# Attention and a two-layer product on one core: the first tile's transfers and constants reordered, mask products on their own, seven half-size products from tile 7 on

## The chip, the cores and the metric

The kernel runs on one core of one Trainium2 chip. The metric is the device time of one execution in microseconds, the median of several runs. The engines have short names in the profile: PE is TensorE (matmul), PEld its weight load, DVE is VectorE, ACT is ScalarE, POOL is GpSimd, SP is SyncE, which only issues transfers here.

## The reference

What must be computed is an attention with two kinds of heads, followed by two matrix products with a pointwise function between them:

```python
B, H, S, D = 4, 8, 768, 64          # batch, heads, sequence, head dimension
scores = q @ k.T / sqrt(D)
causal = i >= j
stream = causal & ((j < 4) | (i - j < 64))       # 4 sink positions, a window of 64
mask = causal if is_retrieval[h] else stream     # a flag of each head
a = softmax(where(mask, scores, -1e9))
x = (a @ v)  ->  (B * S, H * D) = (3072, 512)    # all heads of a token side by side
h = x @ w_in                                     # 512 -> 2048
g = h - tanh(h)
out = g @ w_out                                  # 2048 -> 512, float32
```

Inputs and output are float32. The flags are data, so the kernel finds out on the chip which heads are of which kind.

## The kernel before

The 3072 tokens are cut into 12 tiles of 256 tokens (`TT`), three tiles to a batch (`NG`), tile t = 3b + g. All matmuls are in float16. For one tile the steps are:

- **Load q, k, v.** The first tile's q and k come over SP in four transfers (`load_first`, two halves of four heads, q and k each) and are cast by `cast_first`. Tiles 1 and 2 come over GpSimd's queue, cast on the way, packed with two tokens to a row (`load_cast`, tile `t16p`), and `in_order` sorts them into `t16`. From tile 3 on, raw float32 tiles come over SP in two halves (`load_raw`, `rawqk`, `rawv`), and GpSimd casts and sorts the heads by kind (`gather`, lines L654 and L690). Both buffers exist twice.
- **Transpose q and k.** Tiles 0 to 2 on PE (`st_T`, L987) with copies out of PSUM (L968 and L970, tile `QK`); from tile 3 on by a transposing transfer on SP (`turn`, L573).
- **Scores** on PE (`st_S`, L1082), one visit for one to three units of a head pair. In tiles 0 and 1 (`MASKS`) the mask is added in PSUM first, by a matmul of the identity with a mask tile `m4` of the head pair (L1071). In later tiles VectorE multiplies the mask in after the exp.
- **Exp** on ScalarE (L1095, tiles `pt` and `ptn`), then the product with v on PE (`st_A`, L1174), the division by the sums on VectorE (L1194, L1206, L1221), and a transposition of the result into `xT`: on PE for tiles 0 and 1 (`st_X`, L1256), by a transfer for the others (`st_X_tile`, L1238).
- **First product**, `H_unit` (L1298): eight units of a tile, each 8 matmuls of 256 columns; tanh on ScalarE (L1310), g on VectorE (L1317).
- **Second product.** Up to tile `ST - 1` in the plain way (`O_group`, L1356): for each half of the tokens 16 matmuls of 512 columns. From tile `ST` = 8 on (`quick`) with seven half-size products instead of eight, after Strassen and Winograd: the sums of weight parts are made once (`combine`, L1396, results in `t2`, in the place of tile 2's `t16p` and `gu`, and in `wout` itself), the sums of parts of g once per tile (`sums`, L1446), `piece` (L1478) is one product of 8 matmuls of 256 columns, and `take`, `fold` and `add` (L1513, L1532, L1543) put the output together; `send` (L1563) stores it. `step` spreads a tile's pieces over the eight units of the next tile's first product by the table `STEPS`; `finale` does it for the last tile.

Nothing of the order on the engines is written out by hand. Each step is recorded by `op` or `dma` with its engine, a cost in ns, what it reads and what it writes. `Plan.run` then plays the plan through with these costs: each engine takes, of the operations that are ready, the one recorded first; transfers share the rings and land after a `lag`; PSUM banks and buffers come free as their users end. The order that comes out is the order in which the instructions are issued, and each engine works in it. Where PE would have nothing to do in the first 18 us of the plan, products on a tile of ones (L1765) fill the gap. The numbers above `program` say where in the sequence of product slots the loads, gathers, attention steps and weight sums are recorded: `CUT1` for batch 1, `LEAD`, `LD` and `GA` (visit, load, gather) for batches 2 and 3, `TWHEN` and `TQ` for the weight sums (when, and in how many parts each), `CASTS`, `TE`, `XE` (which engine copies what), `ORDER` (GpSimd's early transfers).

Of the kernel before, what the change touches and what calls it, by code (L numbers as in the profile page):

```python
# [11 lines left out]
XS = 4096.0  # L12
# [243 lines left out]
def kernel(  # L256
# [12 lines left out]
    nc = tc.nc  # L269
# [102 lines left out]
    FROM = 3  # L372
# [3 lines left out]
    MSE = 'DVE'  # L376
    FRONT = "A40"
    LATE = [('vf', 0, 3, 0)]
    BEHIND = []
    MASKS = 2  # L380
    AH = 60
    TL = (1100, 1500)
    RL = (700, 1000)
    A2 = (3, 6)
    ORDER = ('t1', 0, 'v1', 1, 2, 4, 3, 5, 't2', 'r3', 6, 7)

    def program(first):
# [56 lines left out]
        def batch(b):  # L444
            if b in QKs:
                return
            QKs[b], v1s[b], vfs[b], kcs[b] = (buf(x)[0] for x in ("QK", "v1", "vf", "kc"))
            op(
                "POOL", 190, lambda: nc.gpsimd.memset(v1s[b]()[:, :, :, D : D + 1], 1.0 / XS),
                w=[("v1", b, blk, x) for blk in range(2 * NG) for x in range(2)],  # L450
            )
# [5 lines left out]
        def load_first():  # L457

            batch(0)
            rq, iq = buf("rawqk")  # L460
            c, ic = buf("t16")
            raws[0], t16s[0] = (rq, iq), (c, ic)
            r4 = lambda: rq()[:].rearrange("p (x h e) -> p x h e", x=2, h=H)
            for half in range(2):
                hs = slice(half * HH, half * HH + HH)
                for x, src in enumerate((q, k)):
                    dma(
                        "SP", 520,
                        lambda x=x, src=src, hs=hs: nc.sync.dma_start(
                            out=r4()[:, x, hs, :],  # L470
                            in_=src[0, hs, 0:TT, :].rearrange("h (p i) d -> p h (i d)", i=2),
                        ),
                        128 * HH, 26.0, w=[("rawqk", iq, x, half)], lag=(700, 1000),
                    )

# [24 lines left out]
        def load_v(t):  # L500

            b, g = divmod(t, NG)
            for i in range(NB):
                blk = g * NB + i
                dma(
                    "POOL", 900,
                    lambda i=i, blk=blk: nc.gpsimd.dma_start(  # L507
                        out=v1s[b]()[:, blk, :, 0:D],
                        in_=v[b, :, blk * 128 : blk * 128 + 128, :].rearrange("h p d -> p h d"),
                    ),  # L510
                    128 * H, 15.5, w=[("v1", b, blk, x) for x in range(2)],
                )

        def load_cast(t):
# [22 lines left out]
            for x, src in enumerate((q, k)):  # L537
                dma(
                    "POOL", 950,
                    lambda x=x, src=src: nc.gpsimd.dma_start(  # L540
                        out=pk()[:].rearrange("p (x h e) -> p x h e", x=2, h=H)[:, x, :, :],
                        in_=src[b, :, g * TT : (g + 1) * TT, :].rearrange(
                            "h (p i) d -> p h (i d)", i=2
                        ),
                    ),
                    128 * H, 22.6, w=[("t16p", ip, x)],
                )
# [5 lines left out]
        def in_order(t):  # L553

            (pk, ip), (c, ic) = packed[t], t16s[t]
            for x in range(2):
                op(
                    "DVE", 500,
                    lambda x=x: nc.vector.tensor_copy(
                        out=c()[:].rearrange("p (x i h d) -> p x i h d", x=2, i=2, h=H)[:, x],  # L560
                        in_=pk()[:].rearrange("p (x h i d) -> p x i h d", x=2, h=H, i=2)[:, x],
                    ),
                    r=[("t16p", ip, x)] + (BEHIND if t == 1 and first else []),
                    w=[("t16", ic, x, half) for half in range(2)], port=True,
                )

# [51 lines left out]
        def load_w_in(j):  # L618
            dma(
                "POOL", 780,  # L620
                lambda: nc.gpsimd.dma_start(  # L621
                    out=w_in_t[j][:],
                    in_=moe_w_in[:, j * 512 : (j + 1) * 512].rearrange("(cb p) f -> p cb f", p=128),
                ),
                512, 78.0, w=[("win", j)],
            )

        def load_w_out(half, part):
# [8 lines left out]
                ),  # L637
                1024, 43.0, w=[("wout", half, part)],
            )
# [111 lines left out]

        def select(m, src, fill, base, step, mult, key, cmp=ALU.is_ge):
            op(
                "POOL", 300,
                lambda: nc.gpsimd.affine_select(
                    out=m, in_=src, compare_op=cmp, fill=fill,
                    base=base, pattern=[[step, 128]], channel_multiplier=mult,
                ),
                r=["ones", key], w=[key],
            )  # L760

        def rank_constants():
            op(
                "POOL", 300,
# [4 lines left out]
                ),  # L769
                r=["ones"], w=["upto"],  # L770
            )

            select(mS[64:128, 3, :], ones[64:128, :], 0.0, window_i - 65, -1, 1, "mS3")
            select(mS[0:64, 3, :], ones[0:64, :], 0.0, n_sink_i - 1, 0, -1, "mS3")


        def constants():
# [248 lines left out]
        def st_S(units):  # L1026

            todo, reads, keys, ns = [], [], [], 160
            for n, gi in units:
# [28 lines left out]
                if gi == 0 and t < MASKS:  # L1058
                    reads.append(("m4", hp))
                    ns += 2 * o * 0.427 + 100  # L1060
                todo.append((n, gi, b, g, hp, near, sc, key, pieces, o))

            def mm():
                for n, gi, b, g, hp, near, sc, key, pieces, wid in todo:
                    QK = QKs[b]()
                    added = gi == 0 and n // HP < MASKS
                    for hh in range(2) if added else ():
                        m = m4[:, 2 * hp + hh, 0:384]
                        if g:
                            m = m4[:, 2 * hp + hh, 256:512].unsqueeze(1).to_broadcast([128, 2, 256])  # L1070
                        nc.tensor.matmul(  # L1071
                            out=sc()[:, hh, 0:wid], lhsT=ident16[:], rhs=m, start=True, stop=False,
                        )
                    for jb, q0, nb, o, comp in pieces:
# [381 lines left out]
        def piece(t, p, beside=None):  # L1456
# [11 lines left out]
                7: (S(3), T(3), summed(2) + both(3)),  # L1468
            }[p]
            po, key = outs[t, p] = outs[t, beside] if beside else bank(  # L1470
                [128, DM], FP32, "one", f"p{t}_{p}"
# [100 lines left out]
        def step(t, i):  # L1572

            for what in STEPS.get(i, ()):
                if what == "a":
# [15 lines left out]
        def finale(t):  # L1591
# [3 lines left out]
            piece(t, 4)  # L1595
            take(t, 4, "F", 0, CM)
            piece(t, 2)
            fold(t, 2, "A", 0, "E", 0, CM)
# [69 lines left out]
        if first:  # L1668
# [128 lines left out]
        if first and fast:  # L1797
            spread_over([by_rank], BR, BR)
            qs = quads()
            spread_over(qs[: 4 * TQ], slot_of[TWHEN[0]], slot_of[TWHEN[1]])  # L1800
            spread_over(qs[4 * TQ :], slot_of[TWHEN[2]], slot_of[TWHEN[2]])
        spread_over(att_pairs(1) + [lambda: scale_v(1, SV)], 0, 0)
# [3 lines left out]
        def point(h):  # L1806
            t, ts = divmod(h, 2)
            return slot_of[t, 4 * ts + 3] if t >= 2 else max(0, 13 + 2 * h)

# [69 lines left out]
        if quick(last):  # L1879
            sums(last)  # L1880
            finale(last)
        else:
# [46 lines left out]
```

## Time and profile before

| what | value |
|---|---|
| three runs | 229.57, 229.90, 230.34 us, median 229.9 us |
| profiled execution | 230.39 us, span from the first to the last instruction 228.7 us |
| granted TensorE clock, mean | 0.995 |
| PE, DVE, ACT, POOL busy | 95%, 72%, 62%, 47% of the span |
| mean rate of the transfers | 154 GB/s |

Times in the profile are microseconds from the span's start, unless marked ns. A row of the timeline gives start, length, engine, line, operation, output<-input and shape; the brackets at its end say how long the engine sat idle before it and what released it. A row of a group gives the count, the busy time, the mean of one in ns, and the idle time before them. A row of the chain of waits gives start, length, engine and line of one piece. Matmuls overlap in the array, so a row of x8 can be longer than the time it takes up in the chain. SPq, POOLq and ACTq rows are transfers being issued, not their data.

### The profile page before, as it was taken

How to read it: one execution, taken by the hardware profiler on the slowest of the kernel's cores; microseconds unless marked ns; L12 is line 12 of the kernel's file. 1: busy time of each engine (PE TensorE's matmuls, PEld its weight loads, DVE VectorE, ACT ScalarE, POOL GpSimd, SP SyncE). 2: the span in 40 equal slices, each digit the busy share in tenths (PEclk: the TensorE clock that was granted, in tenths of full speed). 3: DMA queues.
4: the chain of work that ended last, by engine and by line, in shares of the span. 5: the costliest groups of instructions: out<-in, count | busy, mean ns of one | idle time of the engine just before them, and what ended most of it. 6: DMA issues, size and time to landing. Idle time of an engine off the chain costs nothing.

```text
span 228.7 us, 6301 instructions
## 1 busy us (share of the span) xinstructions
PE 217.4 (95%) x2373; PEld 163.0 (71%) x2373; DVE 165.7 (72%) x401; ACT 140.8 (62%) x219; POOL 108.4 (47%) x241
## 2 busy tenths in 40 slices
PE   6889999999998989999999999999999999999991
PEld 2356787788985666765765767675868889888880
DVE  5777867775674954999986565476789599684891
ACT  3739849977466847746376657655883766732620
POOL 8999343764741908769473919381000021032020
PEclk9999999999999999999999999999999999999997
DMA  5999999999999989999999989947031022022032
GB/s 164 152 190 204 202 193 218 216 176 248 194 180 217 175 171 239 190 249 174 254 184 220 244 201 215 216 107 162 3 92 49 0 49 93 3 47 95 0 108 84
DMA packets 103876, 35.31 MB, mean 154 GB/s; under 512 B 90658, under 2 KB 101922, under 8 KB 103842
## 3 DMA queue, kind: packets, MB, share of 16 engines
q1 hardware_dynamic: 86544, 27.14, 60.5%
q0 software_dynamic: 17152, 7.60, 25.5%
q8 instruction: 19, 0.31, 0.6%
q14 instruction: 15, 0.12, 0.2%
q10 hardware_dynamic: 146, 0.13, 0.2%
HBM read 27.26 MB, written 6.29 MB: 147 GB/s over the span
## 4 chain that ended last, share of the span: by engine, by line
PE 65%; DMA 14%; POOL 8%; ACT 3%; DVE 3%; SPq 3%; issue 2%; POOLq 0%; DVEq 0%
PE banks L1298 26%; PE banks L1356 19%; PE banks L1478 10%; DMA wout<-in_moe_w_out_dram 7%; PE banks L1082 5%; PE banks L1174 5%; DMA rawqk<-in_k_dram 4%; DMA QK<-t 2%; POOL t L654 2%; POOL v L507 2%; ACT pt L1095 2%; SPq L573 1%; POOL win L621 1%; SPq L609 1%; POOL t16p L540 1%
## 5 line engine op out<-in xcount | busy, mean ns | idle before, releaser
L1298 PE MATMUL banks<-xT,win 128*128 128x256 f16 x768 | 94.8, 273 | 0.5 <-DVE gt L1317 0.4
L1298 PEld LDWEIGHTS <-win 128*128 128x128 f16 x768 | 73.0, 98 | 15.9 <-issue 1.6
L1310 ACT ACTIVATE th<-banks 128x512 f32<-128x512 f32 x96 | 57.2, 605 | 38.7 <-PE banks L1298 38.3
L1317 DVE SCALAR_TENSOR_TENSOR gt<-th,banks 128x512 f16<-128x512 f32 x88 | 59.5, 681 | 18.3 <-ACT th L1310 17.3
L1095 ACT ACTIVATE pt<-banks 128x768 f16<-128x768 f32 (+1 forms) x60 | 53.0, 922 | 10.8 <-PE banks L1082 10.5
L1356 PE MATMUL banks<-wout,gt 128*128 128x512 f16 (+1 forms) x288 | 57.0, 332 | 0.2 <-DMA wout<-in_moe_w_out_dram 0.2
L654 POOL CAST t<-rawqk 128x256 f16 x72 | 28.5, 443 | 31.1 <-DMA rawqk<-in_k_dram 24.8
L1356 PEld LDWEIGHTS <-gt 128*128 128x128 f16 x288 | 25.8, 98 | 14.1 <-issue 1.4
L1543 POOL TENSOR_TENSOR ot<-gu,ot 128x256 f32<-128x256 f32 x6 | 4.5, 752 | 56.4 <-ACT gu L1513 41.8
L1206 DVE TENSOR_TENSOR x16t<-banks,rinv 128x128 f32 (+1 forms) x80 | 22.4, 285 | 1.1
L1082 PE MATMUL banks<-QK 64*128 64x128 f16 (+1 forms) x364 | 21.0, 238 | 1.9 <-DMA QK<-t 1.2
L690 POOL CAST v<-rawv 128x128 f16 x72 | 22.3, 356 | 0.0
L1082 PEld LDWEIGHTS <-QK 64*128 64x128 f16 x364 | 12.8, 94 | 10.9 <-issue 8.1
L1095 ACT ACTIVATE ptn<-banks 128x1024 f16<-128x1024 f32 (+1 forms) x18 | 17.2, 953 | 3.6 <-DVE x16t L1206 2.4
L1174 PEld LDWEIGHTS <-pt 128*128 128x128 f16 x420 | 15.9, 97 | 4.4 <-ACT pt L1095 1.1
L1174 PE MATMUL banks<-v,pt 128*128 128x65 f16 x220 | 16.4, 193 | 0.4 <-DVE pt L1145 0.2
L1145 DVE TENSOR_TENSOR pt<-pt,m4r 128x1024 f16<-128x1024 f16 (+1 forms) x18 | 12.5, 694 | 5.8 <-ACT pt L1095 5.8
L1330 ACT ACTIVATE ot<-banks 128x512 f32<-128x512 f32 (+1 forms) x20 | 10.5, 524 | 9.2 <-PE banks L1356 7.9
L1117 DVE TENSOR_TENSOR ptn<-ptn,mS 128x1024 f16<-128x1024 f16 x12 | 9.6, 803 | 7.6 <-ACT ptn L1095 7.4
L1478 PEld LDWEIGHTS <-m 128*128 128x128 f16 x128 | 12.2, 98 | 1.7 <-issue 0.2
L1174 PE MATMUL banks<-vf,pt 128*128 128x65 f16 x200 | 13.1, 193 | 0.3 <-ACT pt L1095 0.3
L1194 DVE RECIPROCAL rinv<-banks 128x4 f32<-128x4 f32 x48 | 8.1, 174 | 5.6 <-PE banks L1174 5.0
(105 smaller groups left out, 234.7 us busy)
## 6 DMA issues: line engine op xcount, KB each, us to landing
rawqk<-in_q_dram SPq DMA_DIRECT2D x18, 256.0 KB, 4.1
rawqk<-in_k_dram SPq DMA_DIRECT2D x18, 256.0 KB, 4.6
out_dram<-ot SPq DMA_DIRECT2D x18, 256.0 KB, 2.6
rawv<-in_v_dram SPq DMA_DIRECT2D x16, 256.0 KB, 4.8
win<-in_moe_w_in_dram POOLq DMA_DIRECT2D x4, 512.0 KB, 10.7
wout<-in_moe_w_out_dram POOLq DMA_DIRECT2D x4, 512.0 KB, 13.0
out_dram<-ot SPq DMA_DIRECT2D x11, 128.0 KB, 4.0
v<-in_v_dram POOLq DMA_DIRECT2D x6, 128.0 KB, 8.1
```

The lines of the kernel that those rows point to most:

```text
L654: nc.gpsimd.tensor_copy(out=c5()[:, :, :, s_ : s_ + 1, :], in_=r5()[:, :, :, at, :])
L690: nc.gpsimd.tensor_copy(out=v1s[b]()[:, g * NB : g * NB + NB, RANK[s_] : RANK[s_] + 1, 0:D], in_=rv()[:, :, at, :],)
L1082: nc.tensor.matmul(out=sc()[:, hh, o : o + nb * 128], lhsT=lhsT, rhs=QK[p_, hp, q_0 : q_0 + nb * 128], start=not added, stop=not added or ...
L1095: lambda pt=pt, sc=sc, gi=gi, wid=wid: nc.scalar.activation(out=pt()[:, :, 512 * gi : 512 * gi + wid], in_=sc()[:, :, 0:wid], func=AF.Exp, ...
L1145: nc.vector.tensor_mul(out=pv, in0=pv, in1=m)
L1174: nc.tensor.matmul(out=av()[:, i, hh, :], lhsT=pt()[:, hh, co : co + 128], rhs=vv, start=(jb == first_jb), stop=(jb == qb),)
L1206: nc.vector.tensor_mul(out=xt()[:, :, at, :], in0=av()[:, :, hh : hh + 1, 0:D], in1=rinv()[:, :, hh : hh + 1].unsqueeze(3).to_broadcast([1 ...
L1298: nc.tensor.matmul(out=ph()[:, j, :], lhsT=w_in_t[fb // 4][:, cb, f0 : f0 + 128], rhs=x, start=(cb == 0), stop=(cb == HP - 1),)
L1310: lambda: nc.scalar.activation(out=th()[:], in_=ph()[:], func=AF.Tanh, scale=1.0 / XS),
L1317: lambda: nc.vector.scalar_tensor_tensor(out=gt()[:, u * FU : (u + 1) * FU, :], in0=th()[:], scalar=-XS, in1=ph()[:], op0=ALU.mult, op1=AL ...
L1356: nc.tensor.matmul(out=po()[:, c0:c1], lhsT=gt()[:, f, ts * 128 : ts * 128 + 128], rhs=w_out_t[:, f, c0:c1], start=(f == 0), stop=(f == NF ...
L1478: nc.tensor.matmul(out=po()[:, at : at + CM], lhsT=lhs(c), rhs=rhs(c), start=c == 0, stop=c == NC - 1,)
```

## The change

- **Half-size products from tile 7** (`ST` 8 to 7, `TG` 4 to 5), the weight sums in eight parts each instead of four (`TQ`), recorded over another stretch (`TWHEN`); `STEPS` is shifted to units 2, 4, 5, 7, and the last tiles get a table of their own, `STEPL`. The tail function used is the old one under the name `finale_b`; its last but one transfer goes to ScalarE's queue (`ENDS`). A second form, `finale`, is there and not used (`FIN` = 0).
- **Mask products on their own.** The matmul that adds the mask in tiles 0 and 1 is recorded as an operation ahead of the scores, not inside it.
- **First tile.** `constants()` is recorded before `load_first()`; the fourth transfer (k, second half) is issued by ScalarE after its warm-up; both casts of the second half are VectorE's; batch 0's column of constants in v is set by VectorE, batch 1's later; the identity is made after the mask tiles, the rank constants after the first cast.
- **Early transfers.** In GpSimd's queue the first quarter of w_in is put ahead of tile 1's q and k (`ORDER`); tile 1's sorting casts are four on ScalarE instead of two on VectorE, tile 2's four on VectorE.
- **Plan.** Other landing times for several transfers (`WL`, `RL`), `AH` 60 to 0, `LEAD` 3 to 4, `GA` 10 to 12, another `CUT1`, `A2`, `TE`, `XE`: the order of all engines is planned anew from these.

```diff
-    TE = (('DA', 'AA', 'AD', 'DD'), ('DD', 'DD', 'DA', 'DD'), ('AA', 'AD', 'AA', 'DD'))
-    XE = ('DDAD', 'ADDD')
+    TE = (('DA', 'AA', 'AD', 'DD'), ('DD', 'DD', 'DD', 'DD'), ('AA', 'AD', 'AA', 'DD'))
+    XE = ('DADA', 'ADDD')
-    CASTS = (('ACT', 'DVE'), ('ACT', 'ACT'))
+    CASTS = (('ACT','DVE'),('DVE','DVE'))
-    CUT1 = (-8.0, -7.0, 3.0, 14.5)
+    CUT1 = (-9.0, -5.0, 2.25, 13.0)
-    ST = 8
-    TQ = 4
-    TG = 4
+    ST = 7
+    TQ = 8
+    TG = 5
-    TWHEN = ((6, 0), (8, 0), (9, 1))
-    STEPS = {1: (1, 4, "a"), 3: (2, 6, "e"), 5: (5, "b"), 7: (3, 7, "f")}
+    TWHEN = ((4, 0), (8, 0), (8, 1))
+    STEPS = {2:(1, 4, "a"),4:( 2, 6, "e"), 5: (5, "b"), 7:(3, 7, "f")}
+    STEPL = {1: (1, 4, "a"), 3: (2, 6, "e"), 7: (5, "b", 3, 7, "f")}
-    LEAD = 3
+    LEAD = 4
+    FIN = 0
+    ENDS = "ACT"
-    GA = 10
+    GA = 12
+    KRING = ("SS", "SA")
+    IE = ("ACT", "ACT")
+    WL = (1100, 1900)
-    AH = 60
-    RL = (700, 1000)
-    A2 = (3, 6)
-    ORDER = ('t1', 0, 'v1', 1, 2, 4, 3, 5, 't2', 'r3', 6, 7)
+    AH = 0
+    RL = (1100, 1500)
+    A2 = (5, 7)
+    ORDER = (0, 't1', 'v1', 1, 2, 4, 3, 5, 't2', 'r3', 6, 7)
...
@@ batch: the constant column of v
-                "POOL", 190, lambda: nc.gpsimd.memset(v1s[b]()[:, :, :, D : D + 1], 1.0 / XS),
+                "POOL" if b else "DVE", 310 if b else 150,
...
+                r=["regsPOOL"] if b and first else [],
@@ load_first
+                    ring = "ACT" if KRING[half][x] == "A" else "SP"
...
+                        r=["warm"] if ring == "ACT" and half else [],
@@ in_order: four casts instead of two
+                for half in range(2):
+                    e = IE[half] if first and t == 1 else "DVE"
...
@@ rank_constants
+            AT = [("t16", t16s[0][1], 0, 0)]
-                r=["ones"], w=["upto"],
+                r=["ones", *AT], w=["upto"],
@@ constants: the identity last
-            select(ident16[:], ones[:], 0.0, 0, 1, -1, "ident", ALU.is_equal)
...
+            select(ident16[:], ones[:], 0.0, 0, 1, -1, "ident", ALU.is_equal)
@@ st_S
-                    reads.append(("m4", hp))
-                    ns += 2 * o * 0.427 + 100
+                    def add(n=n, g=g, hp=hp, sc=sc, wid=o):
+                        for hh in range(2):
...
+                            nc.tensor.matmul(
+                                out=sc()[:, hh, 0:wid], lhsT=ident16[:], rhs=m, start=True, stop=False,
+                            )
+                    op("PE", 2 * o * 0.427 + 60, add, r=[("m4", hp), "ident"] + ["visit"] * (t > 0), w=[key])
@@ step
-            for what in STEPS.get(i, ()):
+            for what in (STEPS if t < NTT - 2 else STEPL).get(i, ()):
@@ finale_b (finale before)
-            send(t, "F", CM, DM, lambda rows: rows[:, 1, CM:DM])
+            send(t, "F", CM, DM, lambda rows: rows[:, 1, CM:DM], ENDS)
@@ the start of the program
+            constants()
             load_first()
-            constants()
```

More of the change, by code (lines that the diff above doesn't have):

```diff
@@ L448, in batch @@
             op(
-                "POOL", 190, lambda: nc.gpsimd.memset(v1s[b]()[:, :, :, D : D + 1], 1.0 / XS),
+                "POOL" if b else "DVE", 310 if b else 150,
+                lambda: engs["POOL" if b else "DVE"].memset(
+                    v1s[b]()[:, :, :, D : D + 1], 1.0 / XS
+                ),
+                r=["regsPOOL"] if b and first else [],
                 w=[("v1", b, blk, x) for blk in range(2 * NG) for x in range(2)],
@@ L511, in load_v @@
                     128 * H, 15.5, w=[("v1", b, blk, x) for x in range(2)],
+                    lag=(1100, 1800) if t == 0 else WL,
                 )
@@ L545, in load_cast @@
                     ),
-                    128 * H, 22.6, w=[("t16p", ip, x)],
+                    128 * H, 24.0, w=[("t16p", ip, x)], lag=(1100, 2000) if t < 2 else WL,
                 )
@@ L556, in in_order @@
             for x in range(2):
[L557 to L565, printed above, removed]
+                for half in range(2):
+                    hs = slice(half * HH, half * HH + HH)
+                    e = IE[half] if first and t == 1 else "DVE"
+                    op(
+                        e, {"DVE": 400, "ACT": 600}[e],
+                        lambda x=x, hs=hs, e=e: copy(
+                            e,
+                            c()[:].rearrange("p (x i h d) -> p x i h d", x=2, i=2, h=H)[
+                                :, x, :, hs
+                            ],
+                            pk()[:].rearrange("p (x h i d) -> p x i h d", x=2, h=H, i=2)[
+                                :, x, :, hs
+                            ],
+                        ),
+                        r=[("t16p", ip, x)] + (BEHIND if t == 1 and first else []),
+                        w=[("t16", ic, x, half)], port=e == "DVE",
+                    )
         def turn(t, i):
@@ L624, in load_w_in @@
                 ),
-                512, 78.0, w=[("win", j)],
+                512, 78.0, w=[("win", j)], lag=WL,
             )
@@ L637, in load_w_out @@
                 ),
-                1024, 43.0, w=[("wout", half, part)],
+                1024, 43.0, w=[("wout", half, part)], lag=WL,
             )
@@ L750, in scale_v, with select @@
                 )
-        def select(m, src, fill, base, step, mult, key, cmp=ALU.is_ge):
+        def select(m, src, fill, base, step, mult, key, cmp=ALU.is_ge, after=()):
             op(
-                "POOL", 300,
+                "POOL", 310,
                 lambda: nc.gpsimd.affine_select(
@@ L758, in select @@
                 ),
-                r=["ones", key], w=[key],
+                r=["ones", key, *after], w=[key],
             )
         def rank_constants():
+            AT = [("t16", t16s[0][1], 0, 0)]
             op(
@@ L1066, in mm @@
                     added = gi == 0 and n // HP < MASKS
[L1067 to L1073, printed above, removed]
                     for jb, q0, nb, o, comp in pieces:
@@ L1469, in piece @@
             }[p]
+            assert all(k in P.writer for k in r), (t, p)
             po, key = outs[t, p] = outs[t, beside] if beside else bank(
@@ L1596, in finale, with finale_b @@
             take(t, 4, "F", 0, CM)
+            piece(t, 6)
+            fold(t, 6, "A", 0, "E", CM, CM)
+            add(t, "POOL", "tensor_add", ("F", 0), ("E", CM), ("F", 0))
+            piece(t, 7)
+            fold(t, 7, "F", 0, "F", 0, CM, -1.0)
+            send(t, "F", 0, CM, lambda rows: rows[:, 1, 0:CM])
+            piece(t, 5)
+            fold(t, 5, "E", CM, "A", CM, CM, 1.0, ALU.subtract)
+            fold(t, 7, "A", CM, "F", CM, CM)
+            send(t, "F", CM, DM, lambda rows: rows[:, 1, CM:DM])
+            piece(t, 3)
+            fold(t, 3, "A", CM, "E", CM, CM)
+            send(t, "E", CM, DM, lambda rows: rows[:, 0, CM:DM], ENDS)
+            piece(t, 2)
+            fold(t, 2, "A", 0, "E", 0, CM)
+            send(t, "E", 0, CM, lambda rows: rows[:, 0, 0:CM], "ACT")
+        def finale_b(t):
+            piece(t, 1)
+            take(t, 1, "A", 0, CM)
+            piece(t, 4)
+            take(t, 4, "F", 0, CM)
             piece(t, 2)
@@ L1880, in program @@
             sums(last)
-            finale(last)
+            (finale if FIN else finale_b)(last)
         else:
```

15 lines of the change are left out of this document (10 added, 5 removed).

## The prediction

> **What bounds the kernel now.** First the page's first part, then the busy time by stretch (columns: stretch, its length, busy PE, PEld, DVE, ACT, POOL, then clock, DMA share, GB/s).
>
> ```profile
> PE 217.4 (95%) x2373; PEld 163.0 (71%) x2373; DVE 165.7 (72%) x401; ACT 140.8 (62%) x219; POOL 108.4 (47%) x241
> ```
> ```profile
> 100.00:120.00 20.00, 19.71 (x185) 13.17 (x184) 18.30 (x43) 11.33 (x18) 15.30 (x37) 1.00 1.16 213
> 140.00:160.00 20.00, 20.00 (x219) 13.49 (x216) 12.73 (x35) 11.84 (x19) 10.83 (x32) 1.00 0.85 166
> ```
>
> TensorE bounds it. Even in the stretch where VectorE is fullest (18.30 of 20 us), PE idles only 0.29 us. So in the body an edit counts by the product time that it takes out or puts in, and by the waits it brings. Only two places are different: the front, where PE still waits for the first tiles, and the tail after the last product. I go through the four: product work, front, body, tail. The profiled execution took 230.39 us around a span of 228.7; the median of the three runs is 229.9. I add up changes and take them off the median, since the profiled one lies 0.5 above it.
>
> **Product work.** Tile 7's output now comes from seven half-size products of 8 matmuls of 256 columns where 32 matmuls of 512 columns stood. The chain of waits has both kinds, back to back:
>
> ```profile
> 99.91 0.86 PE banks L1356 x4
> ...
> 178.66 0.87 PE banks L1478 x8
> ```
>
> Before: 8 x 0.86 = 6.88 us. After: 7 x 0.87 = 6.09. That is -0.79 us, on PE, where nothing covers it. All other products are in both orders in the same number; only filler products on ones differ.
>
> The price is VectorE's. Its groups by shape:
>
> ```profile
> L1446 DVE TENSOR_TENSOR m<-gt 128x512 f16<-128x512 f16 x16 | 7.4, 475 | 0.1
> ...
> L1396 DVE TENSOR_TENSOR t16p<-wout,t 128x512 f16<-128x512 f16 x4 | 2.4, 609 | 0.0
> ...
> L1396 DVE TENSOR_TENSOR wout<-wout 128x512 f16<-128x512 f16 x4 | 1.6, 414 | 0.0
> ```
>
> Tile 7 adds eight sums of its g at 0.475: 3.8 us, plus two folds that I size by the slowest of these rows, 1.2 us. They fall where tile 8 is multiplied, about 140 to 160, where VectorE had 12.73 us of work: 17.7 of 20. That is less than the 18.30 beside which PE idled 0.29, so I take the cover as enough; without it PE would wait for up to 5 us. The weight sums become 40 of half the size instead of 20. At half of 0.414 plus a fixed part that I bound between 0 and 0.1 us they cost 8.3 to 12.3 us against 8.3 to 12.2 before (20 at 0.414 or 0.609): nothing on balance. In the new order most stand about where they stood; nine stand earlier, behind tile 2's third mask.
>
> **Front.** The mask products now are operations of their own, so two pairs' masks are added before their scores, and both score visits follow each other. PE's and then ScalarE's timeline:
>
> ```profile
> 8.16 0.34 PE L1082 MATMUL banks<-QK 64*128 64x256 f16 x4 [0.73 <-ACT QK L968]
> 8.44 0.71 PE L987 MATMUL banks<-ident,t 128*128 128x128 f16 x8
> 8.98 0.49 PE L1071 MATMUL banks<-m,ident 128*128 128x384 f16 x2
> 9.40 0.34 PE L1082 MATMUL banks<-QK 64*128 64x256 f16 x4
> ```
> ```profile
> 7.95 0.63 ACT L968 CAST t<-rawqk 128x512 f16<-128x512 f32 x1
> 8.55 0.81 ACT L1095 ACTIVATE pt<-banks 128x768 f16<-128x768 f32 x1
> 9.25 0.44 ACT L968 COPY QK<-banks 128x256 f16<-128x256 f16 x1
> 9.78 0.81 ACT L1095 ACTIVATE pt<-banks 128x768 f16<-128x768 f32 x1
> 10.89 1.58 ACT L1095 ACTIVATE pt<-banks 128x768 f16<-128x768 f32 x2 [0.29 <-PE banks L1082]
> ```
>
> The second visit waits from 8.16 to 9.40 behind eight transposes and a mask. In the new order it can start near 8.4. ScalarE loses the cast at 7.95 (VectorE does it now), so its exps can run from about 8.2: four at 0.8 and one copy of 0.44, done near 11.8 instead of 12.47. That is 0.65 us earlier. The cost: VectorE gets that cast and the other of the second half (each at most ScalarE's 0.63) ahead of three mask tiles. What is late next is the key of the second half; before, its cast stood at 7.95, so I take it as landed by then. Its issue moves to ScalarE's queue behind the warm-up; that saves SP one issue, and I cost it at nothing.
>
> Now the trade in GpSimd's queue. Its rows in order of time, the time to landing of the last two, and the group of its small memsets:
>
> ```profile
> 5.54 0.94 POOL L540 DMA_DIRECT2D t16p<-in_q_dram  x1
> 6.47 0.88 POOL L540 DMA_DIRECT2D t16p<-in_k_dram  x1
> 7.33 0.77 POOL L621 DMA_DIRECT2D win<-in_moe_w_in_dram  x1
> ```
> ```profile
> win<-in_moe_w_in_dram POOLq DMA_DIRECT2D x1, 512.0 KB, 7.7
> t16p<-in_k_dram POOLq DMA_DIRECT2D x1, 256.0 KB, 6.1
> ```
> ```profile
> L449 POOL MEMSET v<- 128x48 f16 x4 | 1.2, 312 | 1.1 <-PE banks L1174 0.6 <-POOLq L1910 0.4
> ```
>
> Before, tile 1's key landed at 6.47 + 6.1 = 12.6 and the first quarter of w_in at 7.33 + 7.7 = 15.0. The two change places in the queue. The bytes ahead of the later one stay the same, so I put tile 1's key at 15.0 and w_in near 12.5. Four small instructions (two such memsets, two selects that I size like them) leave the head of this queue: 4 x 0.31 = 1.2 us, about 1.0 if they overlap a little, as an upper bound of what both land earlier. The waits that this part adds cost nothing: the batch 1 memset (0.31) now stands behind the load of the ranks with tile 3's values queued after it, and the two selects behind the first cast with w_in's last quarter after them, but each stands where its release is long past. PE's timeline shows where that is felt:
>
> ```profile
> 14.70 0.29 PE L1256 MATMUL banks<-ident,x 128*128 128x128 f16 x2
> ...
> 15.67 0.56 PE L1082 MATMUL banks<-QK 64*128 64x256 f16 x10
> ```
> ```profile
> 19.37 0.28 PE L1082 MATMUL banks<-QK 64*128 64x256 f16 x2
> ```
>
> New order: last transpose of tile 0's output, then one and a half units of the first product (12 matmuls, 1.3 us at 0.87 for eight), then tile 1's transposes, then its scores. The exps end near 11.8, and VectorE no longer casts tile 1 between, so the last transpose comes near 13.0 instead of 14.70 and the products run from about 13.7. Tile 1's key is cast by ScalarE, 15.0 to 15.6; eight transposes take 0.71, two copies of 0.44 follow, and the first scores of tile 1 come at about 17.1, against 15.67. That is later, but the units that stood behind them are done. Then 0.56 of scores, the other transposes (0.7), four product matmuls (0.4): the second score visit at about 19.05, against 19.37, with four product matmuls more (0.44) and six probability products less (about 0.2) behind it. Gain 0.3 + 0.25 = 0.55 us. Bounds: 1.0 more if the earlier queue head reaches tile 1's key; a loss of 0.9 if the key lands 1.45 us later than 15.0.
>
> **Body.** At 0.87 for eight matmuls of 256 columns, the new order has 5.2 us less product work ahead of the second score visit of tiles 6 to 8, the first that needs tile 7. Chain, SP and POOL rows:
>
> ```profile
> 113.95 0.66 PE banks L1082 x16
> ```
> ```profile
> 103.55 3.61 SPq L573 DMA_TRANSPOSE QK<-t  x2
> ```
> ```profile
> 109.16 0.29 POOL L679 COPY kc<-QK 128x128 f16<-128x128 f16 x1 [0.37 <-DMA QK<-t]
> ```
>
> The visit was at 113.95, and tile 7's transposed tiles had landed by 109.16. Asked for at 113.95 - 5.2 - 0.55 = 108.2, they would be 1.0 us late at the old pace. But the pace changes: the loop gather, transpose issue, second half of the next load, landing, gather is serial, and in it one step had a foreign wait:
>
> ```profile
> 60.95 2.67 SPq L1238 DMA_TRANSPOSE xT<-x16t  x1
> 63.72 2.64 SPq L573 DMA_TRANSPOSE QK<-t  x2
> ```
> ```profile
> 58.80 2.81 POOL L654 CAST t<-rawqk 128x256 f16 x8 [4.47 <-DVE ptn L1111]
> ...
> 73.62 3.73 POOL L654 CAST t<-rawqk 128x256 f16 x8 [3.38 <-DMA rawqk<-in_k_dram]
> ```
>
> Tile 4's casts end at 61.6, yet its transposes issue at 63.72, behind an output tile's. In the new order they stand ahead of that one and of half a load: up to 2.1 us won. I set the late visit against this: body 0, between -0.6 (the 0.29 of idle PE in a stretch of 20 us, twice) and +1.0.
>
> The Trainium skill, page "SBUF — State Buffer", section "Who interferes with whom", says that a VectorE instruction with two inputs in SBUF and a GpSimd instruction that reads SBUF exclude each other, and the second waits for the whole of the first. The trace agrees: the same sum takes 609 ns while GpSimd casts and 414 where it is idle. By that rule smaller sums mean twice as many meetings, which speaks against this change (third rival).
>
> **Tail.** Both last output transfers go to ScalarE's queue.
>
> ```profile
> 223.57 0.42 DVE L1532 SCALAR_TENSOR_TENSOR ot<-banks,gu 128x256 f32<-128x256 f32 x1
> ```
> ```profile
> 224.03 0.39 ACTq L1563 DMA_DIRECT2D out_dram<-ot  x1
> ```
>
> The fold for the other transfer ends where this one starts (223.57), so its issue of 0.39 ends at about 224.0, just when the last one wants the queue. Cost 0, at most 0.4.
>
> **Sum.** -0.79 - 0.55 + 0 + 0 = -1.34 us: 229.9 - 1.3 = 228.6 us (the profiled time would go from 230.39 to 229.05).
>
> **Rivals.**
> 1. *More.* The earlier head of GpSimd's queue reaches tile 1's key (another -0.85 of the 1.0). For it: that queue issues back to back in the rows above. Against: what lands is set by the bytes in the rings, and an earlier issue adds none of their speed. 229.9 - 2.2 = 227.7.
> 2. *Nothing.* Tile 1's key lands 1.3 us after 15.0, because casting transfers of w_in share the rings longer than a swap of places says; every later PE instruction stands behind tile 1's transposes. It eats both gains: 229.9.
> 3. *Slower.* Tile 7 late for the moved-up visit. The sums that now meet GpSimd more often stretch the two gathers that were short (2.81 instead of 3.73) by 0.92 each, the won 2.1 us on SP is lost behind other transfers, and the visit waits 1.0 + 1.8 = 2.8 us: 229.9 - 1.3 + 2.8 = 231.4. It decides from 2.0 us of PE wait there. For it: the loop is serial and the visit is moved by 5 us. Against: most sums stand as late as before, and SP's new order favours the loop.
> That the change does not do what it says is excluded by the new order: the 56 half-size products of tile 7 and the separate masks stand in it.
>
> **Numbers.** Forecast 0.57, more 0.13, nothing 0.14, slower 0.16. The predicted time is the forecast's, 228.6. The low end takes in the second case and its spread, 227.0; the high end takes in the case of nothing and the start of the slower one, 230.4, and leaves out most of that. About 0.3% (0.7 us) is what a measurement tells from no change. Faster: nearly all of the forecast, all of "more", a fifth of "nothing": 0.70. Same: 0.14. Slower: 0.16.
>
> **What would show it.** Right: PE 0.8 us less in products of the second matrix; the second pair's scores within 0.5 us of the first's; first product of tile 0 near 13.7; tile 1's casts on ScalarE ending near 16; no wait of PE on DMA QK around 97 to 110. Wrong: PE waiting for ScalarE's casts beyond 17, a wait over 1 us at tile 6's or 7's scores, or VectorE busy all of the stretch of tile 8 with PE waiting for folds or sums.

## The result and the profile after

The changed kernel takes 236.7 us (median of six runs, 236.0 to 237.5) where the kernel before takes 230.1 (six runs, 228.9 to 231.0): a ratio of 1.029, 95% interval 1.025 to 1.033. Forecast were 228.6 us, with 230.4 as the high end; the kernel became slower. In the profiled execution the span went from 228.7 to 234.3 us.

TensorE's waits by what ended them (us in total, times, longest) have one new entry of a size that matters:

```profile
PE banks L1322 <- ACT ot L1354: 4.8, 1, 4.8
PE banks L1813 <- POOL ones L800: 1.1, 1, 1.1
PE banks L1106 <- ACT QK L990: 1.0, 2, 0.7
```

L1354 is ScalarE's evacuation of an output tile out of PSUM (L1330 before). The chain of waits around that place (start, length, what) says what held it:

```profile
33.55 0.49 ACT th L1334
34.04 0.00 issue
34.04 0.39 ACT ot L1354
34.43 0.02 issue
34.44 7.96 DMA out_dram<-ot
42.41 0.02 issue
42.43 0.04 ACTq L1354
42.47 0.04 issue
42.51 0.39 ACT ot L1354
42.90 0.04 issue
42.95 3.52 PE banks L1322 x16
```

The store of the first evacuated half output tile is issued at 34.44 and lands 7.96 us later. Only then does the second evacuation start. ScalarE's timeline at that place:

```profile
34.04 0.38 ACT L1354 ACTIVATE ot<-banks 128x256 f32<-128x256 f32 x1
35.73 0.60 ACT L1334 ACTIVATE th<-banks 128x512 f32<-128x512 f32 x1 [1.31 <-PE banks L1322]
36.22 0.75 ACT L990 COPY QK<-banks 128x256 f16<-128x256 f16 x2
42.51 0.38 ACT L1354 ACTIVATE ot<-banks 128x256 f32<-128x256 f32 x1 [5.54 <-DMA out_dram<-ot]
42.79 0.44 ACT L990 COPY QK<-banks 128x256 f16<-128x256 f16 x1
43.09 1.73 ACT L1119 ACTIVATE pt<-banks 128x1024 f16<-128x1024 f32 x2
```

ScalarE works in order, so the copies, exps and tanhs queued behind the evacuation stand still for 5.54 us, and with them TensorE's PSUM banks. TensorE's timeline and the two stretches that hold the place (columns as in the prediction's second view):

```profile
37.52 0.62 PE L1009 MATMUL banks<-ident,t 128*128 128x128 f16 x8
42.95 3.50 PE L1322 MATMUL banks<-xT,win 128*128 128x256 f16 x16 [4.81 <-ACT ot L1354]
46.38 0.61 PE L1106 MATMUL banks<-QK 64*128 64x256 f16 x10
```
```profile
30.00:40.00 10.00, 7.47 (x82) 6.42 (x80) 4.40 (x12) 3.31 (x7) 4.19 (x5) 0.97 1.27 218
40.00:50.00 10.00, 7.05 (x72) 5.36 (x73) 4.82 (x9) 6.83 (x12) 7.70 (x21) 0.69 1.29 209
```

The loss has two pieces: TensorE idles 4.81 us, and the 16 products after it take 3.50 us at a granted clock of 0.69 in that stretch.

**Why one evacuation waits for the other's store.** There are three places for output tiles. The plan gives a new one the lowest-numbered place that it takes to be free. By the plan's own times the second evacuation stood 2.09 us after the first before the change, and the store was still on its way, so it got the second place. With the new order it stands 2.77 us behind. The plan has the store land 2.23 us after its issue (the issue, a start and a landing `lag` of 500 and 800 ns, and the bytes), where the trace shows 7.96. So it takes the first place to be free again, by 0.04 us, and reuses it, with two others empty. No view shows this directly, since buffer numbers are left out of the names; experiments 1 and 2 show it.

### The profile page after: what moved, and what is told of

It reads as the page before. It is cut to its first block, busy times and chain, and to the rows that moved or that the text cites. A ratio compares the mean times of both kernels' runs of the same rounds, so it can differ in the third digit from the quotient of the medians.

```text
span 234.3 us, 6407 instructions
## 1 busy us (share of the span) xinstructions
PE 219.9 (94%) x2401; PEld 166.3 (71%) x2401; DVE 172.3 (74%) x434; ACT 142.0 (61%) x221; POOL 112.0 (48%) x243
## 4 chain that ended last, share of the span: by engine, by line
PE 81%; DVE 7%; DMA 5%; ACT 3%; issue 1%; SPq 0%; ACTq 0%
PE banks L1322 34%; PE banks L1380 19%; PE banks L1503 13%; PE banks L1198 7%; PE banks L1106 6%; DMA out_dram<-ot 3%; DMA rawqk<-in_k_dram 2%; DVE gt L1341 2%; DVE QK L992 2%; ACT th L1334 1%; DVE t L1420 1%; ACT pt L1119 1%; PE banks L1087 1%; DVE ptn L1135 1%; ACT QK L990 1%
## 5 line engine op out<-in xcount | busy, mean ns | idle before, releaser
L1322 PE MATMUL banks<-xT,win 128*128 128x256 f16 x768 | 98.6, 276 | 4.8 <-ACT ot L1354 4.8
L1380 PE MATMUL banks<-wout,gt 128*128 128x256 f16 (+1 forms) x256 | 49.5, 326 | 0.5 <-DVE gt L1341 0.5
L1568 POOL TENSOR_TENSOR ot<-gu,ot 128x256 f32<-128x256 f32 x8 | 6.6, 830 | 52.4 <-ACT gu L1538 33.1
L1380 PEld LDWEIGHTS <-gt 128*128 128x128 f16 x256 | 23.0, 98 | 11.4 <-issue 1.8
L1119 ACT ACTIVATE ptn<-banks 128x1024 f16<-128x1024 f32 (+1 forms) x18 | 17.1, 952 | 4.7 <-PE banks L1106 4.7
L1169 DVE TENSOR_TENSOR pt<-pt,m4r 128x1024 f16<-128x1024 f16 (+1 forms) x18 | 14.3, 794 | 4.2 <-ACT pt L1119 4.2
L1503 PEld LDWEIGHTS <-m 128*128 128x128 f16 x160 | 15.4, 98 | 2.0 <-issue 0.2
L1354 ACT ACTIVATE ot<-banks 128x512 f32<-128x512 f32 (+1 forms) x18 | 9.1, 507 | 9.8 <-DMA out_dram<-ot 5.5
L1141 DVE TENSOR_TENSOR ptn<-ptn,mS 128x1024 f16<-128x1024 f16 x12 | 9.0, 752 | 7.7 <-ACT ptn L1119 7.7
```

The lines of the kernel that those rows point to most:

```text
L1119: lambda pt=pt, sc=sc, gi=gi, wid=wid: nc.scalar.activation(out=pt()[:, :, 512 * gi : 512 * gi + wid], in_=sc()[:, :, 0:wid], func=AF.Exp, ...
L1169: nc.vector.tensor_mul(out=pv, in0=pv, in1=m)
L1322: nc.tensor.matmul(out=ph()[:, j, :], lhsT=w_in_t[fb // 4][:, cb, f0 : f0 + 128], rhs=x, start=(cb == 0), stop=(cb == HP - 1),)
L1380: nc.tensor.matmul(out=po()[:, c0:c1], lhsT=gt()[:, f, ts * 128 : ts * 128 + 128], rhs=w_out_t[:, f, c0:c1], start=(f == 0), stop=(f == NF ...
L1503: nc.tensor.matmul(out=po()[:, at : at + CM], lhsT=lhs(c), rhs=rhs(c), start=c == 0, stop=c == NC - 1,)
```

## The experiments

**1. Another place for the second output tile.** Nothing else changes; the order on all engines is the same.

```diff
-        self.end = max(self.done)
+        self.end = max(self.done); self.bank_of["ot", 1] = (2,)
```

> The changed kernel, every instruction in the same order on every engine; only the second output tile of tile 0 is put into the third place of the ot buffers instead of the first. Theory A (the place is the loss): the second evacuation no longer waits 5.54 us on ScalarE for the first store, TensorE's wait of 4.81 us near 38 to 43 goes, the 16 products after it take 1.9 us instead of 3.50 at a granted clock of 1.0, about 0.5 us of smaller waits go too; with the changed kernel at 236.7 us this one comes to 229.0 to 230.0, or to 228.6 if the prediction's other terms hold in full (ratio to before 0.993 to 0.999). The first store itself still takes about 8 us to land. Rival B (the transfers of this stretch are the loss, and the place only where it shows): GpSimd's casting loads land as late as they did, so TensorE gets a wait of 3 to 5 us on another transfer between 38 and 50, the time stays at 234 to 237 and the clock still falls. Rival C (the loss lies in the order after 50 us, where visits are moved up): the wait goes, but later waits grow by as much; 234 to 236.

228.5 us (eight runs, 228.3 to 229.4); ratio 0.9912, interval 0.988 to 0.9943. The prediction's ratio was 228.6 / 229.9 = 0.9943. ScalarE's and TensorE's timelines:

```profile
36.80 0.75 ACT L990 COPY QK<-banks 128x256 f16<-128x256 f16 x2
37.38 0.41 ACT L1354 ACTIVATE ot<-banks 128x256 f32<-128x256 f32 x1
```
```profile
38.55 1.91 PE L1322 MATMUL banks<-xT,win 128*128 128x256 f16 x16
```

The wait is gone and the same 16 products take 1.91 us. The first store still lands after 7.6 us, but the second evacuation no longer waits for it. Rivals B and C fall.

**2. The kernel before with the shared place**, in the same manner: `self.bank_of["ot", 1] = (0,)`.

> The kernel before, every instruction in the same order; only the second output tile of tile 0 is put into the first place of the ot buffers, as in the changed kernel. Theory A: the evacuation at 36.32 us waits for the first store (issued at 34.54, landing 7.7 us later), so until about 42.3; ScalarE loses 6.0 us and TensorE, which still has some 1 to 2.5 us of products to do, waits 3.5 to 5 us and then runs 1 to 2 us at a lower clock: 230.1 + 5 to 7 = 235 to 237. Rivals B and C: the place by itself costs under 1 us, because the transfers or the order elsewhere set the time: 230 to 231.

236.5 us (235.8 to 237.1); ratio 1.025, interval 1.021 to 1.030, so one buffer number gives the kernel before the bulk of the loss. Its ScalarE and TensorE:

```profile
42.35 0.38 ACT L1330 ACTIVATE ot<-banks 128x256 f32<-128x256 f32 x1 [5.73 <-DMA out_dram<-ot]
```
```profile
43.70 1.31 PE L1082 MATMUL banks<-QK 64*128 64x256 f16 x10 [4.71 <-ACT pt L1095]
44.95 3.60 PE L1298 MATMUL banks<-xT,win 128*128 128x256 f16 x16
```

**3. Why the store takes 8 us: its queue?** The changed kernel with the first store issued by ScalarE.

```diff
-                lambda: engs[ring].dma_start(out=out[t0 : t0 + 128, c0:c1], ...
+                lambda: engs["ACT" if (t, ts, c0) == (0, 0, 0) else ring].dma_start(...
```

> The changed kernel with the shared place; the only difference is that the first store of tile 0 is issued in ScalarE's queue right behind its evacuation instead of in SP's. What holds the store for 8 us? Theory (the DMA engines work off what GpSimd's casting loads put in before it): it lands as late, 7 to 8 us after its issue, and the time stays at 236 to 237. Rival (something of SP's queue holds it): it lands in 2 to 4 us as the later stores do, the second evacuation waits 1 to 2 us instead of 5.54, TensorE's wait falls under 1.5 us and its clock stays at 1.0: 230 to 231.

235.8 us (four runs, 234.5 to 237.4); ratio 1.023, interval 1.018 to 1.029. The store lands 7.8 us after its issue and the second evacuation waits 5.40 us. It is not SP's queue.

**4. What stands ahead of it?** The changed kernel, where GpSimd clears the second halves of w_out with a memset; their values are left out.

```diff
-                lambda: nc.gpsimd.dma_start(
+                lambda: nc.gpsimd.memset(w_out_t[...], 0.0) if half else nc.gpsimd.dma_start(
```

> The changed kernel with the shared place; the last two casting loads of GpSimd's queue ahead of the first store (512 KB each, the second halves of w_out, issued at 32.56 and 34.13) are left out and those parts of w_out set to zero by GpSimd instead. Everything else in the same order. Theory (casting loads ahead of the store hold it): the store still has tile 4's three loads of 256 KB before it, so it lands after 3 to 5 us instead of 8.0, the second evacuation waits 0.5 to 2.5 us, TensorE loses 3 to 5.5 us less: 231 to 234. Rival (a store behind this stretch takes 8 us whatever is loaded): 236 to 237.

232.4 us (ten runs, 231.7 to 234.5); ratio 1.009, interval 1.005 to 1.012. The store lands after 5.9 us, more than the 3 to 5 expected; the evacuation waits 2.36 us:

```profile
40.80 0.38 ACT L1354 ACTIVATE ot<-banks 128x256 f32<-128x256 f32 x1 [2.36 <-DMA out_dram<-ot]
```
```profile
41.23 1.91 PE L1322 MATMUL banks<-xT,win 128*128 128x256 f16 x16 [1.63 <-ACT ot L1354]
```

So casting loads ahead of the store are part of its 8 us. The memsets take 3.57 us on GpSimd and TensorE waits 1.4 us for VectorE beside them, so the time is not a pure measure of the store. In the profiled run a TensorE wait of 1.63 us leaves the clock alone (1.00 in both stretches). That run is the shortest of the ten; in five others the mean granted clock is 0.988 or less and the time 232.6 to 234.5 us, and why is not shown.

**5. The base for the parts.** The changed kernel with every output tile in the place longest free (one key more where the plan chooses), in the same order.

```diff
-  key=lambda z: (max(z[0], t), -z[1][0] if k[0] == "one" else z[1][0])
+  key=lambda z: (max(z[0], t), z[0] if k[0] == "ot" else 0, -z[1][0] if k[0] == "one" else z[1][0])
```

> The changed kernel, every instruction in the same order, but every output tile goes to the place of the ot buffers that has been free longest in the plan (before: the lowest-numbered free one). This is the base for the three runs beside it. If only the first reuse counted, 228.5 like the kernel with just the second tile moved; the few other waits for a store (under 0.3 us each) may be worth up to 0.3 us more: 228.2 to 228.6. If waits for stores were the loss all along the body, 227 or less.

228.7 us (228.3 to 229.0); ratio 0.9899, interval 0.9858 to 0.9939: like experiment 1. Only the first reuse cost.

**6 to 9. One part of the change undone, each on that base.** The plan is played anew each time, so later work moves too.

```diff
6   ST = 8; TQ = 4; TG = 4; TWHEN, STEPS as before
7   the two mask matmuls inside the scores' operation again
8   ORDER = ('t1', 0, 'v1', ...
9   LEAD = 3; GA = 10
```

> The kernel with the longest-free places, with the half-size products from tile 8 on again and the weight sums in four parts, as before. The prediction's product term: 7 x 0.87 = 6.09 us of products for tile 7 become 32 of 512 columns, 6.88 us, so +0.8 us: 229.3. Rival (the sums on VectorE cost what the products saved, or the gain lies elsewhere): no difference, 228.5, with less waiting of TensorE on VectorE.

> The kernel with the longest-free places, with the mask products inside the scores again. The prediction's front term: the second score visit stands behind eight transposes and a mask again, 0.6 to 1 us later, and the exps, the last transpose of tile 0's output and the first product with it; +0.3 to +0.6 us at the end: 228.8 to 229.1. Rival (the front is set by the landing of tile 1's key and of w_in, not by the exps): no difference, 228.5.

> The kernel with the longest-free places, with tile 1's q and k ahead of w_in's first quarter in GpSimd's queue, as before. The prediction had this trade at nothing: the key lands about 2 us earlier and the quarter of w_in about 2 us later, near 15, so the first product starts 0.5 to 1 us later and tile 1's scores up to 1 us earlier: 228.1 to 229.0, so within 0.5 us. Rival (the trade is what makes the front better): 229.5 or more, with TensorE waiting for w_in near 14 to 16.

> The kernel with the longest-free places, with the visits, loads and gathers of batches 2 and 3 recorded where they stood before (LEAD 3, GA 10). The prediction put the body at nothing, between -0.6 and +1.0: 228.7 +- 0.4. Its third rival (tile 7 late for the moved-up visit) would make this one faster than the kernel with the longest-free places, 227 to 228; were the moved-up visits a gain, it is slower, 229.3 or more, with waits of TensorE on the transposed tiles near 100.

| undone | median, range | ratio, interval | against the base |
|---|---|---|---|
| 6: half-size products of tile 7 | 230.1, 229.5 to 230.9 | 0.9966, 0.994 to 0.9992 | +1.4 us |
| 7: masks apart | 229.9, 229.5 to 230.4 | 0.9949, 0.9922 to 0.9976 | +1.2 us |
| 8: w_in ahead of tile 1's key | 229.0, 228.6 to 229.7 | 0.9912, 0.9879 to 0.9946 | +0.3 us |
| 9: visits and gathers as before | 231.0, 230.4 to 232.6 | 1.0023, 0.9997 to 1.0049 | +2.9 us |

The runs of 6 and 7, on the base's chip, do not overlap with its 228.3 to 229.0; those of 8 do. Number 9 ran on another chip, so its difference is taken over the ratios, whose intervals do not overlap: 1.0023 - 0.9899 of 230.9 us (the medians differ by 2.3).

**10 to 12. One part alone in the kernel before**, with the places longest free: that rule by itself, masks apart, half-size products from tile 7.

```diff
10  the key of number 5
11  the same, and the mask matmuls as an operation ahead of the scores
12  the same as 10, and ST = 7; TQ = 8; TG = 5; TWHEN, STEPS, STEPL as changed
```

> The kernel before, every instruction in the same order, every output tile in the place longest free. Base for the run beside it and for the one with the masks apart. The waits for stores in the kernel before were 1.0 us on ScalarE, not on the path of TensorE: no difference, ratio 0.998 to 1.001. Were stores a loss before as well, 229 or less.

> The kernel before with the mask products as operations of their own and nothing else of the change (output tiles in the place longest free, so that no store is waited for). The prediction's front term without the moved casts: -0.3 to -0.6 us against before, ratio 0.997 to 0.9985. Rival (the masks apart pay only with the casts moved to VectorE and the other order of transfers): no difference, ratio 0.999 to 1.001.

> The kernel before with the half-size products from tile 7 on (weight sums in eight parts, steps shifted) and nothing else of the change; output tiles in the place longest free. The prediction's product term: -0.79 us, ratio 0.9965 (0.9955 to 0.9975). If undoing it in the changed kernel (+1.4 us) measured the products alone, -1.4 us, ratio 0.994. Rival (the part pays only with the order that the rest of the change gives): ratio 0.999 to 1.002, with waits of TensorE on VectorE or on transposed tiles in place of the products.

Ratios 1.0014 (0.9989 to 1.0039), 0.999 (0.9967 to 1.0014) and 1.0011 (0.9984 to 1.0039): none of them changes the time by what these runs can tell. The half-size products are in the last one, and TensorE's waits suggest where their gain went:

```profile
PE banks L1299 <- DMA xT<-x16t: 1.3, 1, 1.3
PE banks L1083 <- DMA QK<-t: 0.8, 1, 0.8
...
PE banks L1479 <- ACT gu L1514: 0.5, 1, 0.5
```

Transposing transfers hold TensorE for 2.1 us, against 1.5 in the profile of experiment 10 and 1.2 in the kernel before, and an evacuation into gu for 0.5. The wait for xT, the transposed output of attention, is new; the waits for QK did not grow.

## Why the prediction was wrong

**The step that failed** is that the new order's waits were put at nothing without looking at what an evacuation waits for. It is not one of the terms that the prediction weighed: the parts on the front and the body move the evacuations of tile 0's output, and cost TensorE's order, the transposed tiles and SP's order, but not what an evacuation itself waits for. "The waits that this part adds cost nothing" counted GpSimd's waits only. The wait that came in is of ScalarE for a buffer, about 4.8 us of idle TensorE and 1.6 us (3.50 - 1.91) of products at a lower clock; with 0.4 us more idle time between 60 and 220, that is nearly all of the 7.2 us by which TensorE's last product ends later than in the base with the same order (229.21 against 222.05). Experiments 1 and 2 show it from both sides. None of the three rivals was this. The third one, slower, has the right sign by luck: its mechanism, a late tile 7, does not show in the changed kernel, where TensorE's waits list none for QK's transposing transfers. The wait that came would have had its data in the trace of before: the first store was issued at 34.5 and took 7.7 us to land, and the second evacuation on ScalarE started 2.2 us after the first.

```profile
34.13 0.38 ACT L1330 ACTIVATE ot<-banks 128x256 f32<-128x256 f32 x1
36.32 0.45 ACT L1330 ACTIVATE ot<-banks 128x256 f32<-128x256 f32 x1
```
```profile
DMA to landing us min/median/max: 1.7/3.1/7.7
```

**Without that wait the sum was about right, but its terms were not.** The base (experiment 5) against the kernel before: TensorE's last product ends at 222.05 instead of 223.54, -1.5 us, where -1.3 was forecast; the medians differ by 2.3, with an interval of 1.4 to 3.3. That the sum comes near is luck: a gain in the body, put at nothing, stands in for the front's, which did not come.

- *Product work*, forecast -0.79. In the base's chain 80 matmuls of the half-size products stand back to back:

```profile
213.29 8.77 PE banks L1503 x80
```

  That is 0.877 us for eight, so tile 7's seven cost 6.14 us in place of 6.88: -0.74. The size was right. VectorE's cover held as well: in the base it has 15.95 us of work from 140 to 160 (17.7 forecast) and 18.48 from 160 to 180, and TensorE idles in neither. The prediction's reading that a sum takes 609 ns beside GpSimd is looser than it says: 609 is the mean of four from 418 to 843 ns, and the one of 418 stands inside GpSimd's casts. Alone the half-size products bring nothing that can be told (experiment 12).
- *Front*, forecast -0.55. The first steps came near to what was told: in the changed kernel the scores of both first pairs are one group at 7.54, the first product is at 14.13 (13.7 forecast), tile 1's first scores are at 16.70 (17.1), and its casts on ScalarE end at 15.8 (near 16). The gain did not follow. The four exps end at 12.27 (11.8 forecast, 12.47 before), and tile 1's second scores, forecast at 19.05 against 19.37 before, come at 19.42, and at 19.86 in the base:

```profile
7.54 0.50 PE L1106 MATMUL banks<-QK 64*128 64x256 f16 x8 [0.28 <-ACT QK L990]
14.13 1.47 PE L1322 MATMUL banks<-xT,win 128*128 128x256 f16 x12
16.70 0.56 PE L1106 MATMUL banks<-QK 64*128 64x256 f16 x10 [0.21 <-DVE QK L992]
19.42 0.56 PE L1106 MATMUL banks<-QK 64*128 64x256 f16 x10
```
```profile
19.86 0.56 PE L1106 MATMUL banks<-QK 64*128 64x256 f16 x10
```

  With the 0.24 us that the prediction allows for the products ahead of it, that is a gain of 0.2 us in the changed kernel and a loss of 0.25 in the base. By the end, what is left in the base after product work and body is -1.49 + 0.74 + 1.21 = +0.5 us, a loss. In the profile of experiment 1, which has the same order and waited 1.6 us for the first tile's casts, it is +1.3 (last product 222.60, no idle time from 60 to 180). From 20 to 60 us TensorE idles 1.27 us in the base against 0.71 before, and these are its longest waits there:

```profile
37.20 0.56 PE L1106 MATMUL banks<-QK 64*128 64x256 f16 x10 [0.67 <-ACT QK L990]
45.18 0.60 PE L1380 MATMUL banks<-wout,gt 128*128 128x256 f16 x4 [0.59 <-DVE gt L1341]
```

  The first stands in the changed kernel and in experiment 1 with the same 0.67. No run takes these waits away by themselves, so how much of the lead they cost is not shown.
- *Body*, forecast 0. It gained. Four stretches, two of the kernel before and two of the base:

```profile
60.00:80.00 20.00, 19.41 (x211) 14.87 (x210) 13.49 (x26) 13.71 (x21) 12.18 (x35) 1.00 1.27 199
80.00:100.00 20.00, 19.39 (x215) 13.50 (x212) 13.88 (x33) 12.81 (x19) 10.61 (x27) 1.00 1.01 204
```
```profile
60.00:80.00 20.00, 20.00 (x229) 15.72 (x226) 14.44 (x33) 13.64 (x21) 10.81 (x31) 1.00 1.11 196
100.00:120.00 20.00, 20.00 (x212) 14.06 (x211) 17.71 (x54) 12.86 (x20) 12.32 (x32) 1.00 1.16 214
```

  Before, TensorE idles 0.59 + 0.61 and, in the stretch shown in the prediction, 0.29 us; in the base 0.28 us in all from 60 to 180. That is -1.2 us, twice the best that the prediction allowed. The serial loop of gather, transpose and load, which it weighed as a risk, shows the gain: its waits on transposed tiles (1.2 us before) are nearly gone (0.3). Which setting removes them is open. The new places of visits and gathers alone do not account for it: experiment 9, with the old ones, idles only 0.37 us in that stretch. What holds TensorE in experiment 12 is the late transposed output, not the late tile 7 of the third rival.
- *Tail*, forecast 0: from the last product to the end of the span 5.2 us before, 4.9 in the base.

The parts do not add up: undoing four of them costs 1.4 + 1.2 + 0.3 + 2.9 = 5.8 us, all together bring 2.3 (231.0 to 228.7), and two of them alone bring nothing that can be told. With the plan played anew, each part moves what the others need. That is shown as times; the waits that replace a gain are seen only in the one profile of experiment 12. For number 9 it stays open: its profile, one of its fastest runs, has TensorE's last product 0.5 us later than the base and 1.1 us more from there to the end, and no wait in the body that would explain the rest.

## What to carry to other kernels

Where a change reorders the work of a planner that also hands out buffers, compare the places it hands out as well as the order: a place that is reused turns a slow store into a wait of a whole in-order engine. Before calling a moved step free, list what it waits for in the trace of before with the time to landing of the slowest transfer, not the planner's figure for it. And a saving of matmul time can be lost to waits in another order, as in experiment 12: measure it in the order in which it will stand.

## What was not expected of the hardware

**A small store behind casting loads.** The first store of 128 KB, issued between 33 and 36 us, needs 7.4 to 9.1 us to land in every kernel here that loads the same, and other stores of output tiles 1.7 us at best. Queue rows of the changed kernel, from just after its issue to 39, and from 40 to 41 (packets, MB, share of 16 engines; q0 has GpSimd's loads, q1 SP's transfers):

```profile
q0 software_dynamic: 293, 0.98, 103.5%
```
```profile
q0 software_dynamic: 215, 0.11, 79.3%
q1 hardware_dynamic: 123, 0.11, 42.4%
```

From 34.5 to 39 not one packet of SP's queue moves; from 39 to 40 it is 13 packets, and then nearly all of the store's 0.13 MB goes in one microsecond. The Trainium skill, page "DMA: Bandwidth & Descriptors", section "Queues, rings and completion order", says that each DMA engine takes packets from its queues in turn. By that rule the store would have begun to move beside the loads; the trace shows 4.5 us without it, whether it is issued by SP or by ScalarE. What orders it behind the loads is not settled here.

**The clock after a wait.** After 4.81 us without work, the changed kernel's 16 products of 256 columns take 3.50 us instead of 1.91, and the rows behind them run at full speed. In experiment 2, after 4.71 us, ten score products take 1.31 us instead of 0.61, and the 16 products behind them 3.60: over 5 us of slow rows. In experiment 3, after 4.67 us, the 16 products take 3.57 and ten score products 0.86. After 1.63 us, in experiment 4, the 16 products take 1.91. The Trainium skill, page "TensorE: Matmul & The Clock Gate", section "Part 1: The HAM clock gate (the "warmup" mystery)", gives an idle window of about 3.4 us after which the clock is halved, and as long a busy one until it is back. The traces agree on the idle side; the slow stretch is that long in the changed kernel (3.43 us) and longer in experiment 2. On top of itself such a wait cost 1.6, 2.7 and 1.9 us in these three profiles, taken from its end to the start of the next group that runs at full speed (3.98 us against 2.39, 5.74 against 3.07, 4.30 against 2.39).
